# A decode block on one Trainium2 core: 128 columns of the first weight load move to a transfer of their own

## The chip, the cores and the metric

The kernel runs on one NeuronCore of one Trainium2 chip. The metric is the device time of one execution in microseconds (us), the median of several runs. A profile is one further execution, taken by the hardware profiler. The core has five instruction engines (PE for matmuls, with PEld for its weight loads; DVE, ACT and POOL for vector work; SP, which here only issues transfers) and 16 DMA engines that carry all data between HBM and the core's SBUF.

## The reference

One decode step for two sequences (B = 2, model width D = 448). The input is layer-normalised, then it goes through attention over a cache (16 query heads, 8 key/value heads, 4096 positions, head width 256) and through a bilinear feed-forward; the attention's output is multiplied by the gate and added to the input. All data are float32.

```python
xn = _layernorm(x)
q = (xn @ wq).reshape(B, 1, 16, 256).transpose(0, 2, 1, 3)
k, v = [jnp.repeat(t, 2, axis=1) for t in (k_cache, v_cache)]      # (2, 8, 4096, 256) each
p = softmax(jnp.einsum("bhqd,bhkd->bhqk", q, k) * 256 ** -0.5)
s = jnp.einsum("bhqk,bhkd->bhqd", p, v).transpose(0, 2, 1, 3).reshape(B, 1, 4096) @ wo
g = silu(((xn @ w_gate) * (xn @ w_up)) @ w_down)                    # inner width 1792
return x + s * g
```

The caches alone are 134 MB, the weights another 24 MB, and each byte is used once.

## The kernel before

**Data.** The host lays every array out as 128 rows, one for each SBUF partition, so that a load is 128 rows of one length. SP issues the loads in a fixed order, written out in `gated_decode_block` as a list of plans (lines 281 to 290): `wq0` (the first half of the query weights, 128 rows of 7168 columns = 28,672 bytes), `wgu` (gate and up weights), `wdq` (down weights and second half of the query weights), `first` (keys of the first head and sequence), then 14 loads `vk` of 128 rows of 65,536 bytes (values of one head and sequence, keys of the next), with `wo` after the second of them, and at the end `last0` in two pieces and `last1` in five, the last three of which are 5, 2 and 1 blocks of 448 columns of the output weights. The first four are issued at once; every later one waits until PE has done with the buffer it overwrites. There are two ring buffers and one slot.

**Work.** `query(0)` multiplies the normalised input by `wq0`: 14 blocks of 512 columns, the helper `rows` takes 12 of them in a first loop and the blocks 12 and 13 in a second one, so that block 13 is read by the last of its matmuls. `ffn_in`, `ffn_out` and `query(1)` follow. Then, for each head and sequence: scores, softmax, values. At the end `project` and `project_last` multiply by the output weights; `project_last` for the last eight chunks reads the last three pieces of `last1` as they land. Two DVE operations and the store of the result close the kernel.

**Recording.** The operations are not issued as they are written. `Recorder` notes them, `Flow.settle` works out from the regions that they read and write which must wait for which, and `Flow.issue` writes them out for each engine, with one semaphore for each transfer. So all instructions stand on the lines of that helper (line 220) in the profile, and are told apart by the tiles' names: `ring<-wq` is the load of `wq0`, `s<-ring,xnT` and `s<-ring,oT` are matmuls of `rows` (and of `project_last`, near the end).

Of the kernel before, what the change touches and what calls it, by code (L numbers as in the profile page):

```python
# [22 lines left out]
EPS = 1e-5  # L23
WQ = 14 * 512
LEAD = 48


class Flow:
# [115 lines left out]
    def issue(self):  # L144
        nc = self.nc
        lead = nc.alloc_semaphore("lead")
        for _ in range(LEAD):
            nc.vector.sem_inc(lead)
# [72 lines left out]
        return add  # L221


def gated_decode_block(nc, x, first, vk, last0, last1, wq0, wdq, wo, wgu, out):
    flow = Flow(nc)
    PE, DVE, ACT, POOL, SP = [getattr(flow, e) for e in ("PE", "DVE", "ACT", "POOL", "SP")]
    names = iter(range(1000))
# [35 lines left out]
    def issue(n=1):  # L263
        for names, place, src, cuts in todo[:n]:
            t = place()
            width = ROW if not names[0].startswith("w") else src.shape[1] // len(names)
            for i, name in enumerate(names):
                loaded[name] = t[:, i * width:(i + 1) * width]
            if names == ["wd", "wq1"]:
                loaded["wd"], loaded["wq1"] = t[:, :14 * D], t[:, 14 * D:]  # L270
            for lo, hi in zip(cuts, cuts[1:]):
                SP.dma_start(t[:, lo:hi], src[:, lo:hi])
        del todo[:n]

    def plan(names, place, src, cuts=None):
# [13 lines left out]
    plan(f"k{LAST + 1} v{LAST}", ring, last0, [0, ROW, 2 * ROW])  # L289
    plan(f"v{LAST + 1} wo2", ring, last1, [0, 6144, ROW, *(ROW + i * D for i in (5, 7, 8))])  # L290
    issue(4)


# [230 lines left out]
    for first in range(0, LAST, B):  # L524
        flow.turn = first
        issue(2)
        if first == 0:
            flow.turn = None
            issue()
            flow.turn = first  # L530
        for i in range(first, first + B):
            p = softmax(i, s)
            o = bank("o")
            values(i, p, o)
            DVE.tensor_copy(ob[:, i % B], o)
            q = copy()
            POOL.tensor_copy(q, query_of(i + 1))
            s = scores(i + 1, q, two())
        total(add_head)
        cb = combine(ob)  # L540
        t = work["h"]()[:, :B * 64]
        DVE.tensor_tensor(t.rearrange("p (s k) -> p s k", s=B), cb.rearrange("p (s k) -> p s k", s=B),
                          over[:, :, None].to_broadcast([128, B, 64]), op=OP.mult)
        turn(oT, first // B, t)
# [19 lines left out]
    t = work["h"]()  # L564
# [62 lines left out]
```

## Time and profile before

| | |
|---|---|
| median of 3 runs | 374.49 us (374.22 to 374.6) |
| the profiled execution's own time | 374.3 us |
| its span, from the first to the last instruction | 372.7 us |
| mean granted TensorE clock | 0.766 of full speed |
| PE busy, DVE busy, ACT busy | 188.0, 75.5, 26.7 us |
| moved by DMA | 158.67 MB, 426 GB/s over the span |

Times in views are counted from the first instruction. The profiled execution's own time is 1.6 us more than its span: work ahead of the first and behind the last instruction. A DMA share is the time of all packets that start in a stretch, divided by 16 engines times the stretch; in a stretch shorter than a packet it goes over 100%, and it then gives the packet's own duration (share x 16 x stretch). Every transfer is cut into packets, here one for each row, plus one packet of 4 bytes on each engine that took part, which counts up the semaphore.

### The profile page before, as it was taken

Reading aid. Unit: us, or ns where it says so; the run is one execution under the profiler, and the core shown is the slowest. Engines: PE = TensorE matmul, PEld = TensorE weight load, DVE = VectorE, ACT = ScalarE, POOL = GpSimd, SP = SyncE. Lnnn points to the kernel's source line nnn. Section 1 sums busy time; section 2 is a strip of 40 time slices with the busy share of each in tenths; the row PEclk is TensorE's granted clock in tenths of the full one; section 3 lists DMA queues with packets and bytes.
Section 4 is the critical chain, followed back from the end, with each engine's and each line's share of the span. In section 5 each row is a group of like instructions: output and inputs, shape, how many; then the busy total and the mean of one; then the engine's idle time right before and its main releaser. Section 6 shows DMA issues by size and latency. Waiting matters only on the chain. (4 is left out here: it accounts for less than half of the span.)

```text
span 372.7 us, 3346 instructions
## 1 busy us (share of the span) xinstructions
PE 188.0 (50%) x1474; PEld 57.2 (15%) x1474; DVE 75.5 (20%) x124; ACT 26.7 (7%) x44; POOL 5.6 (2%) x28
## 2 busy tenths in 40 slices
PE   0818292171900626555453638271919090908786
PEld 0201020020200201111121102020202030202223
DVE  2101013021130030313031212221131304030430
ACT  1101011001010010101000000101010101010121
POOL 0100000000000000000000000000000000000000
PEclk9968598596875685958595958695867586776999
DMA  8999999999999999999999999999999999999995
GB/s 339 466 424 410 429 433 450 443 445 396 425 459 436 450 443 436 429 394 450 436 450 443 436 429 394 450 436 450 443 436 429 394 450 436 450 397 443 421 414 233
DMA packets 3897, 158.67 MB, mean 426 GB/s; under 512 B 562, under 2 KB 692, under 8 KB 820
## 3 DMA queue, kind: packets, MB, share of 16 engines
q1 hardware_dynamic: 3888, 158.59, 98.6%
q8 instruction: 4, 0.07, 0.1%
q14 instruction: 1, 0.01, 0.0%
q10 hardware_dynamic: 4, 0.00, 0.0%
HBM read 158.54 MB, written 0.06 MB: 426 GB/s over the span
## 5 line engine op out<-in xcount | busy, mean ns | idle before, releaser
L220 PE MATMUL o<-ring,pT 128*32 128x512 f32 x480 | 81.4, 840 | 115.3 <-PEq L172 115.3
L220 PE MATMUL s<-ring,qc 128*32 128x512 f32 x448 | 50.7, 592 | 0.0
L220 PEld LDWEIGHTS o<-ring,pT 128*32 128x32 f32 x480 | 20.7, 149 | 163.5 <-issue 163.5
L220 DVE COPY ob<-o 128x512 f32<-128x512 f32 x14 | 9.7, 692 | 155.9 <-PE o L220 155.9
L220 ACT ACTIVATE p<-s,m 128x1024 f32<-128x1024 f32 x16 | 17.8, 1113 | 287.5 <-DVE m L220 287.5
L220 DVE TENSOR_REDUCE m<-s 128x1 f32<-128x1024 f32 x16 | 19.3, 1205 | 21.9 <-PE s L220 21.9
L220 DVE STREAM_TRANSPOSE pT<-p 128x1024 f32<-128x1024 f32 x15 | 18.7, 1245 | 19.1 <-ACT p L220 19.1
L220 PEld LDWEIGHTS s<-ring,qc 128*32 128x32 f32 x448 | 15.1, 110 | 33.0 <-issue 33.0
L220 PE MATMUL sm<-ident,m 128*1 128x128 f32 x16 | 4.3, 269 | 25.6 <-PEq L172 23.7
L220 PE MATMUL s<-ring,xnT 128*32 128x448 f32 (+1 forms) x72 | 12.1, 828 | 8.3 <-DMA ring<-wgu 8.3
L220 DVE TENSOR_REDUCE mx<-sm 1x128 f32<-1x512 f32 x16 | 10.9, 679 | 8.0 <-PE sm L220 8.0
L220 PE MATMUL sm<-one,mx 1*128 1x1 f32 x16 | 3.2, 198 | 12.9 <-PEq L172 12.1
L220 PE MATMUL s<-slot,hT 128*32 128x448 f32 x28 | 5.4, 885 | 8.0 <-DMA slot<-wdq 8.0
L220 POOL COPY qc<-qT 128x64 f32<-128x64 f32 x14 | 3.2, 236 | 290.9 <-PE s L220 283.6
L220 PE MATMUL s<-ring,qT 128*32 128x512 f32 x64 | 7.5, 597 | 0.0
L220 PEld LDWEIGHTS sm<-ident,m 128*1 128x1 f32 x16 | 1.3, 79 | 35.1 <-issue 32.9
L220 DVE RECIPROCAL over<-sm 128x2 f32<-128x2 f32 x8 | 1.4, 170 | 23.9 <-PE sm L220 23.9
L220 PE MATMUL s<-ident,pT 2*128 2x2 f32 x4 | 0.6, 247 | 10.5 <-DVE pT L220 10.5
L220 PE MATMUL cb<-ob,add_blocks 128*32 128x128 f32 x128 | 5.2, 279 | 0.6 <-ACT ob L220 0.6
L220 PEld LDWEIGHTS s<-ring,xnT 128*32 128x32 f32 x72 | 2.6, 145 | 17.0 <-DMA ring<-wgu 9.2
L220 PE MATMUL s<-ring,oT 128*32 128x112 f32 (+2 forms) x76 | 5.1, 314 | 0.1
L220 PE MATMUL wide<-slot,oT 128*32 128x448 f32 x48 | 4.9, 539 | 0.0
(65 smaller groups left out, 60.9 us busy)
## 6 DMA issues: line engine op xcount, KB each, us to landing
ring<-last SPq DMA_DIRECT2D x2, 4096.0 KB, 26.3
slot<-wdq SPq DMA_DIRECT2D x1, 6720.0 KB, 42.2
ring<-wgu SPq DMA_DIRECT2D x1, 6272.0 KB, 26.0
slot<-wo SPq DMA_DIRECT2D x1, 5376.0 KB, 46.6
ring<-first SPq DMA_DIRECT2D x1, 4096.0 KB, 51.2
ring<-wq SPq DMA_DIRECT2D x1, 3584.0 KB, 11.7
ring<-last SPq DMA_DIRECT2D x1, 3072.0 KB, 21.1
ring<-last SPq DMA_DIRECT2D x1, 1120.0 KB, 23.7
```

What stands on the lines that cost most here:

```text
L220: self.flow.record(self.engine, lambda: method(out, *args, **kw), writes, reads, name == "dma_start")
```

## The change

The last 128 of the 7168 columns of `wq0` leave its rows, which become 28,160 bytes long. They come as an array of their own, `wqx`, which is 4 groups of 33 rows of 128 columns, the 33rd row of each group being padding that is never read. Right behind the load of `wq0`, and ahead of `wgu`, SP issues one more transfer: 4 groups of 32 rows of 512 bytes into the same 128 columns of the same tile. Bytes read and their places in SBUF are the same as before.

```diff
+SHARE = 4
+COLS = 128
...
+            if names == ["wq0"]:
+                width = WQ
...
             for lo, hi in zip(cuts, cuts[1:]):
                 SP.dma_start(t[:, lo:hi], src[:, lo:hi])
+            if names == ["wq0"]:
+                SP.dma_start(t[:, cuts[-1]:WQ], wqx[:, :128 // SHARE])
...
     wq0, wq1 = [folded(wq[:, h], 512) for h in range(2)]
+    wqx = np.zeros((SHARE, 128 // SHARE + 1, COLS), np.float32)
+    wqx[:, :-1] = wq0[:, WQ - COLS:].reshape(SHARE, 128 // SHARE, COLS)
+    wq0 = c(wq0[:, :WQ - COLS])
```

## Rows read from the trace of the kernel before

**Rows 1.** Page, DMA busy share in 40 slices (tenths), and the queues.

```profile
DMA  8999999999999999999999999999999999999995
q1 hardware_dynamic: 3888, 158.59, 98.6%
q8 instruction: 4, 0.07, 0.1%
```

**Rows 2.** The chain that ended last, in order of time: start us, us, what.

```profile
344.56 23.68 DMA ring<-last
...
368.28 2.14 PE s L220 x64
...
370.44 0.29 DVE gate L220
```

**Rows 3.** Timeline from 368 us: start us, us, what, in brackets idle before and releaser.

```profile
368.28 0.92 PEld L220 LDWEIGHTS s<-ring,oT 128*32 128x32 f32 x40 [0.34 <-DMA ring<-last]
...
369.43 0.35 PEld L220 LDWEIGHTS s<-ring,oT 128*32 128x32 f32 x16 [0.23 <-DMA ring<-last]
369.97 0.16 PEld L220 LDWEIGHTS s<-ring,oT 128*32 128x32 f32 x8 [0.19 <-DMA ring<-last]
```

**Rows 4.** Windows near the end: stretch, busy by engine, PE clock, DMA share, GB/s.

```profile
366.00:367.50 1.50, 0.94 (x16) 0.25 (x8) 0.00 (x0) 0.68 (x1) 0.00 (x0) 1.00 0.99 400
367.50:368.00 0.50, 0.44 (x16) 0.38 (x16) 0.00 (x0) 0.01 (x1) 0.00 (x0) 1.00 0.98 373
```

**Rows 5.** The same view in shorter stretches behind it.

```profile
368.30:368.50 0.20, 0.20 (x9) 0.20 (x13) 0.20 (x1) 0.00 (x0) 0.00 (x0) 1.00 0.45 179
...
368.70:368.90 0.20, 0.20 (x20) 0.20 (x16) 0.00 (x0) 0.00 (x0) 0.00 (x0) 1.00 0.27 108
...
369.10:369.30 0.20, 0.20 (x16) 0.10 (x5) 0.00 (x0) 0.00 (x0) 0.00 (x0) 1.00 0.25 99
369.30:369.40 0.10, 0.10 (x8) 0.00 (x0) 0.00 (x0) 0.00 (x0) 0.00 (x0) 1.00 0.19 72
...
369.50:369.60 0.10, 0.10 (x8) 0.10 (x12) 0.00 (x0) 0.00 (x0) 0.00 (x0) 1.00 0.01 0
```

**Rows 6.** Queues, 350.2 to 350.3 us: packets, MB, share of 16 engines.

```profile
q8 instruction: 1, 0.02, 55.1%
```

**Rows 7.** Queues, 351.09 to 351.10 us.

```profile
q1 hardware_dynamic: 1, 0.03, 1101.2%
```

**Rows 8.** Queues, 351.14 to 351.16 us.

```profile
q1 hardware_dynamic: 1, 0.03, 379.1%
```

**Rows 9.** Windows, from 200 to 345 us.

```profile
200.00:345.00 145.00, 77.67 (x572) 23.56 (x576) 30.66 (x45) 8.43 (x14) 1.42 (x6) 0.75 0.99 431
```

**Rows 10.** Queues, 371.8 to 373 us: the store, 128 rows of 448 bytes.

```profile
q1 hardware_dynamic: 144, 0.06, 17.2%
```

**Rows 11.** Queues, 369.10 to 369.34 us: rows of 1792 bytes.

```profile
q1 hardware_dynamic: 13, 0.02, 25.1%
```

**Rows 12.** Queues, 5.5 to 6.7 us: q10 carries one row of the input x.

```profile
q10 hardware_dynamic: 2, 0.00, 0.4%
```

**Rows 13.** Timeline of SP's issues.

```profile
0.74 0.38 SPq L220 DMA_DIRECT2D ring<-wq  x1
1.17 0.42 SPq L220 DMA_DIRECT2D ring<-wgu  x1
...
35.89 22.13 SPq L220 DMA_DIRECT2D ring<-vk  x2
```

**Rows 14.** Timeline of PE's weight loads from 12 to 28 us.

```profile
12.71 0.20 PEld L220 LDWEIGHTS s<-ring,xnT 128*32 128x32 f32 x8 [1.29 <-DMA ring<-wq]
...
17.82 0.20 PEld L220 LDWEIGHTS s<-ring,oT 128*64 128x64 f32 x4 [1.50 <-issue]
27.22 0.20 PEld L220 LDWEIGHTS s<-ring,xnT 128*32 128x32 f32 x8 [9.21 <-DMA ring<-wgu]
```

**Rows 15.** Waits of SP: what waited for what, us in total, times, longest.

```profile
SPq L191 <- DMA res<-gate: 1.1, 1, 1.1
```

More of the change, by code (lines that the diff above doesn't have):

```diff
@@ L221, in __getattr__, with gated_decode_block @@
         return add
-def gated_decode_block(nc, x, first, vk, last0, last1, wq0, wdq, wo, wgu, out):
+def gated_decode_block(nc, x, first, vk, last0, last1, wq0, wqx, wdq, wo, wgu, out):
     flow = Flow(nc)
@@ L619 @@
     nc = bacc.Bacc("TRN2", target_bir_lowering=False, num_devices=1, dynamic_dma_scratch_size=1024)
-    arrays = dict(x=x, first=first, vk=vk, last0=last[0], last1=last[1], wq0=wq0, wdq=wdq, wo=wo, wgu=wgu)
+    arrays = dict(x=x, first=first, vk=vk, last0=last[0], last1=last[1], wq0=wq0, wqx=wqx, wdq=wdq, wo=wo, wgu=wgu)
     args = [nc.dram_tensor(n, a.shape, mybir.dt.from_np(a.dtype), kind="ExternalInput").ap()
```

## Prediction

> **What bounds the kernel now.** I read the page's first two parts and its queues, then the chain that ended last, then the end of the timeline, and then the DMA share in short windows, since what ends last turned out to be a transfer.
>
> The 16 DMA engines are the bound: their busy share stands at nine tenths or more in all slices but the first and the last, and SP's queue alone takes 98.6% of the span [rows 1]. PE, with 188 us of 372.7, waits for data. The chain of waits says where the end comes from: it lies on the transfers of `ring<-last` up to 368.23 us, then on the last 64 matmuls and two DVE operations [rows 2]. The timeline shows that these matmuls are still fed by transfers: the weight loads at 369.43 and 369.97 were each released by `ring<-last` [rows 3]. So the end stands at a fixed distance behind the landing of the last row of the last piece.
>
> That row lies on one engine, and the 16 do not end together. Between 366 and 368 us all are busy (share 0.99 and 0.98) [rows 4]. Then the share falls to 0.45, 0.27 and 0.25, which is four engines of 16; to 0.19, three engines, from 369.3 on; and to nothing after 369.5 [rows 5]. So some ten engines have ended by 368.3, four go on for more than a microsecond, one of these ends at about 369.35 and three at about 369.5. Bytes are no reason, since each 128-row transfer gives every engine eight rows. What differs is four packets of instructions, 0.07 MB in all [rows 1]. One of them took 55.1% x 16 x 0.1 us = 0.88 us [rows 6]. A data packet that begins as it ends took 1101.2% x 16 x 0.01 = 1.76 us [rows 7], where its neighbour of the same size took 379.1% x 16 x 0.02 = 1.21 [rows 8]: 0.55 more. Together that is 1.43 us on one engine, and 1.4 is just how far the four lag behind those that end near 368. So four engines each carried one instruction packet, and the kernel ends when the last of them does. That each of the four packets fell on another engine I infer from the four late ends.
>
> **What the change removes.** Each row of `wq0` loses 512 bytes; an engine's eight rows lose 4096. In the long stretch the queue moved 431 GB/s at a share of 0.99 [rows 9], that is 431 / 16 / 0.99 = 27.2 bytes a nanosecond on one engine. So each of the 16 saves 4096 / 27.2 = 0.15 us. Nothing hides this: the streams have no gap in which it could vanish, so an engine that is given nothing back ends 0.15 us sooner.
>
> **What it adds: 128 rows of 512 bytes.** First, on how many engines. The store, 128 rows, shows 144 packets [rows 10]: 128 rows and 16 completions, so 16 engines. One row of `x` shows two [rows 12]: one row and one completion, one engine. The new transfer has 4 groups at its outer level on one side and 128 rows on the other. The bounds are 4 engines with 32 rows each and 16 with eight; I take 4, since the outer count is what decided in both cases that the rows show, and keep 16 as a rival.
>
> The Trainium skill, DMA: Bandwidth & Descriptors, section "Why a DMA increments its semaphore by 16 and not by 1", says that the number of engines is the largest one up to 16 that divides the outer count of both sides, and that they are the lowest-numbered: 4 here, with the engine of the `x` rows among them. The two counts above agree with it; a transfer of 4 groups no row shows. By it the rival of 16 would fall away.
>
> Then, what one row of 512 bytes takes. From below: 512 / 27.2 = 19 ns, a piece of a long row. From above: a row of 1792 bytes, 25.1% x 16 x 0.24 us / 13 = 74 ns [rows 11]. The nearest row is the store's 448 bytes: 17.2% x 16 x 1.2 us / 144 = 23 ns a packet [rows 10], though that one writes to HBM and this one reads. On the line between 448 and 1792 bytes, 512 bytes take 25 ns; I take that. So 32 x 25 = 0.80 us for each of the four engines, net 0.80 - 0.15 = +0.65 us (bounds 0.45 and 2.22). The completion packet is hidden in the rounding.
>
> **What of it lies on the path.** The other 12 engines gain 0.15. If one of the three that end near 369.5 is among the four, the end moves by +0.65; if only the one that ends near 369.35, by about 0.15 less, +0.5. If none of the late four is among them, an engine that ends near 368.1 moves to 368.8, still ahead of the late ones, and the end moves by -0.15. Which four engines it is no view tells, since the rows carry no engine's number. By count alone, the chance that four engines out of 16 miss four given ones is (12 x 11 x 10 x 9) / (16 x 15 x 14 x 13) = 0.27, so 0.73 that a late one is hit.
>
> **What it moves at the start.** SP issues one transfer more, 0.4 us as its neighbours [rows 13], and `wgu` goes out at about 1.6 instead of 1.17. That is hidden behind the load of `wq0`, which lands only shortly before PE begins at 12.71 [rows 14]; without that cover it would cost 0.4. Only block 13 reads the new columns, in the last matmuls of `query(0)`, whose weight load stands at 17.82 [rows 14]; the new transfer lands within a microsecond of the old one. Behind these PE is idle for 9.21 us until `wgu` lands [rows 14], so even a wait there is hidden. `wgu` may land 0.65 us later if its slowest engine is one of the four; then PE, and behind it the issue of the first `vk` at 35.89 [rows 13], come 0.65 later. The queue still holds all of `first` at that time, 128 rows of 8192 columns, 4.2 MB or 9.7 us at 431 GB/s, so no engine runs dry. Later issues wait for PE in the same way, behind a load in flight.
>
> **Sum.** Own time 374.3, plus 0.65, or 0.5 if only the earlier of the late four is hit: 0.6 as a middle, 374.9. The median of the runs stands 0.19 above the profiled execution, so on it the same sum gives 375.1. Changes under 0.2%, 0.75 us, are about what a measurement of this kernel can't tell from none.
>
> **The rivals.**
>
> - *None of the late four is hit* (-0.15): 374.15 on the own time, 374.34 on the median. For it: 12 of 16 engines are early and have 1.2 us to spare [rows 5], more than the 0.65. Against it: 0.27 by count. It would be no measurable change either.
> - *The transfer spreads over 16 engines*, so the change does not do what it says: 8 x 25 ns = 0.20 added and 0.15 removed everywhere, 374.35. For it: the SBUF side still has 128 rows. Against it: the engines went by the count of 1 in the `x` rows.
> - *Slower, by the price of a small read.* If rows of 512 bytes from HBM take as long as those of 1792, 74 ns, a late engine that is hit ends 2.2 us later: 376.5, or +0.6%. An early one would end near 370.2, +0.7 us. This decides as soon as a late engine is hit and a row takes over (0.75 + 0.15) / 32 = 28 ns, or 33 ns on the earlier one, not far from my 25. For it: no row shows a read that small. Against it: the price falls with size down to 448 bytes, if only for writes.
> - *A small transfer stops the queue.* The store took 1.1 us by itself from its issue to its completion [rows 15]. If each engine paused so long around the new transfer, all 16 would lose 1.1 - 0.15: 375.25, slower by 0.25%. Against it: the seven pieces of the end follow each other at shares of 0.99 and 0.98 [rows 4]. The Trainium skill, DMA: Bandwidth & Descriptors, section "Rules for kernel authors", warns that under 64 KB a transfer is mostly overhead, and this one is 64 KB. By its table in "Measured", 64 KB take 0.95 us, which would make the sum 375.1. The trace does not bear that out for transfers queued behind others.
>
> **How the numbers follow.** Late engine hit, at some 25 ns a row: 0.53. None hit: 0.20. Sixteen engines: 0.05. Small reads dear, on a late engine: 0.14. The queue stops: 0.03. What is left, 0.05, is that the instruction packets fall elsewhere, or take less room, in the new program: I give 0.04 of it to a gain over 0.2%, which no price above reaches, and 0.01 to a loss. Faster is then 0.04, within 0.2% 0.53 + 0.20 + 0.05 = 0.78, slower 0.14 + 0.03 + 0.01 = 0.18. The likeliest gives 374.9, with a range of its own from 374.7 to 375.25 (the lower bound of the row's price on the own time; +0.75 on the median). The whole range runs from 374.1, where none is hit, to 375.4, which takes in the stopped queue and the dear reads up to some 33 ns a row.
>
> **What would show it.** In the profile after: some 0.06 MB of packets under 2 KB behind `wq0`, 128 of them with 4 completions (16 if it spreads), in some 25 ns each; the last weight load at 370.5 instead of 369.97 if a late engine is hit, at 369.8 if none is; the share near the end at about four engines still, three of them ending earlier by 0.15. The wait for `wgu` stays in place of any wait for the new transfer. The prediction is wrong if the rows of 512 bytes take over 30 ns, if the instruction packets move to other engines or times, or if the end moves by more than its slowest engine does.

## The result, and the profile after

The median of 22 runs is 374.95 us, beside 374.48 us for 22 runs of the kernel before in the same comparison. The ratio is 1.0041, with a 95% interval from 1.0024 to 1.0058: slower by 0.4%, where no measurable change was forecast. The ratio gives the high runs a weight that they do not have in a median; the two runs at 381.78 and 382.88, over 1.5% above the fastest, count as a slower state and are left out of it. The median lies within 0.05 us of the predicted 374.9, but for another reason. Of the 22 runs 12 lie between 374.46 and 374.97 us, with a median of 374.69; the other ten lie at 378.0 or above (six at 378.0 to 378.3, two near 379, and the two just named). All 22 of the kernel before lie between 374.22 and 375.41. So two things are to be explained: some 0.2 us in the lower runs, and 3.5 us or more in the others.

The profiled execution is one of the first kind: 374.64 us, with a span of 372.9. The lines of the helper stand two lines further down (222 instead of 220). Its queues on the page:

```profile
DMA packets 4029, 158.67 MB, mean 425 GB/s; under 512 B 566, under 2 KB 824, under 8 KB 952
...
q1 hardware_dynamic: 4020, 158.59, 98.6%
```

SP's queue has 4020 packets instead of 3888 [rows 1]: 132 more, 128 rows and 4 completions. So four engines carry the new transfer. Its packets, in a stretch in which only one engine still works on it:

```profile
q1 hardware_dynamic: 15, 0.01, 7.2%
```

That is the queue view from 12.34 to 12.69 us. 7.2% x 16 x 0.35 us / 15 = 27 ns for a packet, and 0.35 / 15 = 23 ns from one start to the next, since each begins a little before its predecessor ends. The price of 25 ns was right for most rows. Twelve of the 128, between 11.58 and 12.34 us, took 61 to 102 ns, most of them on the engine that was last to finish. From 11.85 to 12.30:

```profile
q1 hardware_dynamic: 7, 0.00, 7.7%
```

That is 7.7% x 16 x 0.45 us / 7 = 79 ns. The issues of SP, in its timeline:

```profile
0.74 0.38 SPq L222 DMA_DIRECT2D ring<-wq  x1
1.18 0.69 SPq L222 DMA_DIRECT2D ring<-wqx  x1
1.94 0.64 SPq L222 DMA_DIRECT2D ring<-wgu  x1
2.62 0.52 SPq L222 DMA_DIRECT2D slot<-wdq  x1
```

The new issue takes 0.69 us, not 0.4 as its neighbours did [rows 13], and the next ones are longer too. All of it ends long before `wq0` has landed, so it is hidden. The chain of waits ends as before, on `ring<-last` and the last 64 matmuls [rows 2]:

```profile
344.64 23.98 DMA ring<-last
...
368.66 2.05 PE s L222 x64
...
370.73 0.29 DVE gate L222
```

The last weight load in the timeline stands at 370.26 instead of 369.97 [rows 3], 0.29 later:

```profile
368.66 1.39 PEld L222 LDWEIGHTS s<-ring,oT 128*32 128x32 f32 x56 [0.35 <-DMA ring<-last]
...
370.26 0.16 PEld L222 LDWEIGHTS s<-ring,oT 128*32 128x32 f32 x8 [0.21 <-DMA ring<-last]
```

And the windows near the end, as [rows 4, 5]:

```profile
367.50:368.00 0.50, 0.07 (x4) 0.07 (x8) 0.00 (x0) 0.38 (x1) 0.00 (x0) 1.00 0.90 348
368.30:368.50 0.20, 0.20 (x12) 0.01 (x1) 0.00 (x0) 0.00 (x0) 0.00 (x0) 1.00 0.59 233
368.70:368.90 0.20, 0.20 (x12) 0.20 (x16) 0.20 (x1) 0.00 (x0) 0.00 (x0) 1.00 0.28 108
369.10:369.30 0.20, 0.20 (x20) 0.20 (x13) 0.00 (x0) 0.00 (x0) 0.00 (x0) 1.00 0.32 125
...
369.50:369.60 0.10, 0.10 (x16) 0.08 (x4) 0.00 (x0) 0.00 (x0) 0.00 (x0) 1.00 0.14 54
369.70:369.80 0.10, 0.10 (x12) 0.10 (x8) 0.00 (x0) 0.00 (x0) 0.00 (x0) 1.00 0.09 36
```

The share falls earlier (0.90 where it was 0.98) and ends later: after 369.5, where nothing was left before, two engines still work, and one after 369.7. It looks like the step that was forecast, an engine that ends late and has got more to carry. The packets say otherwise. The queue view names no engine, but a packet begins some 4 ns before the one ahead of it on its engine ends, so the packets of the trace can be strung into 16 sequences. The first row of 512 bytes begins at 10.97 us, so an engine with 32 of them, 23 ns apart, can't be done before 11.70. Four engines begin `wgu` later than that, at 11.73, 11.79, 11.82 and 12.72; they end at 368.68, 368.72, 368.75 and 369.65. The last to end, at 369.95, is none of these: it began `wgu` at 11.48 and carried the instruction packet at 78.45. In the kernel before, the packet at 78.12 fell on an engine that began `wgu` at 11.22, and that one ended last too, at 369.57. The two packets (78.44 to 78.45 us, and before, 78.11 to 78.12):

```profile
q8 instruction: 1, 0.02, 624.4%
q8 instruction: 1, 0.02, 596.2%
```

and the first row of `wgu` on the engine that carried each (11.480 to 11.481, and before, 11.221 to 11.222):

```profile
q1 hardware_dynamic: 1, 0.05, 12006.2%
q1 hardware_dynamic: 1, 0.05, 11581.2%
```

So the end moved because one instruction packet fell on an engine that stood 0.26 us further behind, with a first row of `wgu` 0.07 us longer, and not because the last engine had small rows to carry. Nothing in this trace hints at 378 us.

### The profile page after: what moved, and what is told of

The parts are those of the page before. It is cut to its first block, busy times and chain, and to the rows that moved or that the text cites. A ratio compares the mean times of both kernels' runs of the same rounds, so it can differ in the third digit from the quotient of the medians.

```text
span 372.9 us, 3347 instructions
## 1 busy us (share of the span) xinstructions
PE 192.0 (51%) x1474; PEld 58.1 (16%) x1474; DVE 75.5 (20%) x124; ACT 26.8 (7%) x44; POOL 5.6 (2%) x28
## 3 DMA queue, kind: packets, MB, share of 16 engines
q1 hardware_dynamic: 4020, 158.59, 98.6%
## 5 line engine op out<-in xcount | busy, mean ns | idle before, releaser
L222 PE MATMUL o<-ring,pT 128*32 128x512 f32 x480 | 86.0, 881 | 110.6 <-PEq L174 110.6
L222 PEld LDWEIGHTS o<-ring,pT 128*32 128x32 f32 x480 | 21.5, 154 | 161.5 <-issue 161.5
```

Source lines behind the costliest of these rows:

```text
L222: self.flow.record(self.engine, lambda: method(out, *args, **kw), writes, reads, name == "dma_start")
```

## The experiments

The theories, as the expectations name them. **A**: in some runs the small rows are dear. **B**: in some runs all engines read slower, because arrays lie badly in HBM. **C**: four engines that stand 0.6 us behind the others bring this about. **D**: the sizes of the arrays shift the places of those behind them. **E**: the small rows on few engines bring it about, by whatever means; **E1**: that the engines are few, **E2**: that one engine's small rows are many. Each run of five rounds gives 10 to 12 times; "high" means 377 us or more. The diffs show the lines that matter and leave out the rest. No run of the kernel before, of the 22 and another 155 beside the experiments, was over 375.6.

**The change again, its 16-engine form, another place, eight groups.**

```diff
 e2_sixteen, e12_sixteen_again
+    wqx = c(wq0[:, WQ - COLS:])
+                SP.dma_start(t[:, cuts[-1]:WQ], wqx)
 e3_behind_wgu
-            if names == ["wq0"]:
-                SP.dma_start(t[:, cuts[-1]:WQ], wqx[:, :128 // SHARE])
+            if names == ["wg", "wu"]:
+                SP.dma_start(ring.bufs[1][:, WQ - COLS:WQ], wqx[:, :128 // SHARE])
 e4_eight
-SHARE = 4
+SHARE = 8
```

> The changed kernel once more, unaltered. Of 22 runs of it, 12 lay at 374.5 to 375.0 us and the others at 378 or above, while all 22 of the kernel before lay at 374.2 to 375.4. Theory A (price): in some executions the rows of 512 bytes are read at over 100 ns instead of 24 to 27, so one of the four engines ends some 3.7 us later; runs at 378 come again, in about 4 of 10, and if the profile is of such a run the new transfer's last completion lands near 16 us instead of 13.2. Theory B (rate): the arrays lie elsewhere in HBM, or the engines stand otherwise to each other, and all 16 move data 1% slower through the whole run; then a profile at 378 shows some 421 GB/s in every slice and a landing of the new transfer at 13 us. Rival: the runs at 378 were no property of the kernel; then all lie at 374.5 to 375.0.

Measured: 2 of 11 high (377.87, 378.28), the others with a median of 374.84; ratio 1.0026 (1.0006 to 1.0047). The high runs belong to the kernel.

> The same 128 columns in a transfer of their own at the same place, but as 128 rows of 512 bytes at the outer level, so that 16 engines carry eight rows each. By my sum: 0.2 us added and 0.15 removed on each engine, so 374.5, the kernel before within 0.1%. Theory A: a read of 100 ns costs at most 0.8 us on an engine, so no run over 375.5. Theory B by addresses: the arrays behind wq0 are displaced here too, so runs at 378 come as often as with the change. Theory B by the engines' standing: no run at 378, since all engines are shifted alike.

Measured: 0 of 11 high, 374.56 to 375.70; ratio 1.0016 (1.0007 to 1.0025). The page counts 4032 packets on SP's queue, 144 more than before, so 16 engines.

> The new transfer, unaltered in shape, is issued behind wgu instead of ahead of it, so that the engines read it at 26 us and not at 11, among rows of 53,760 bytes. Last matmuls of query(0) wait until 27 us for it, which PE's idle time there hides. Theory A with a price that comes from the place near the start: no runs at 378, 374.7 to 375.0. Theory A with a price of any small read: runs at 378 as often as with the change. Theory B: as often as with the change.

Measured: 1 of 10 high, at 377.36, the others with a median of 375.0; ratio 1.0024 (1.0010 to 1.0038). The place at the start is not what matters. This one run lies 2.4 us above the others and not 3.5; with only `wdq` behind the small rows that would fit the row times below (8 x 0.24 = 1.9 us), but no profile shows it.

> 8 groups of 16 rows of 512 bytes: by the counts, eight engines carry 16 rows each, 16 x 24 ns = 0.38 us added and 0.15 removed, net +0.23 on these and -0.15 on the other eight. My sum: 374.3 to 374.8. Theory A: at 130 ns a row some runs at 376.3 instead of 378 (half the rows on an engine, half the delay). Theory B: the second group stays at 378.

Measured: 4 of 12 high (378.25, 378.37, 380.35, 382.81), the others with a median of 374.76; ratio 1.0018 (1.0000 to 1.0036). Half the rows on an engine do not halve the delay, against A. The profiled execution is the one at 378.25, with a span of 376.6, and shows where it comes from. From the transfers' view of this kernel (issue to landing, us, at the end of each line):

```profile
q1 hardware_dynamic: 4024, 158.59, 98.5%
...
slot<-wdq SPq DMA_DIRECT2D x1, 6720.0 KB, 44.8
ring<-wgu SPq DMA_DIRECT2D x1, 6272.0 KB, 27.4
...
ring<-first SPq DMA_DIRECT2D x1, 4096.0 KB, 53.8
ring<-wq SPq DMA_DIRECT2D x1, 3520.0 KB, 11.4
```

The same view of the changed kernel:

```profile
slot<-wdq SPq DMA_DIRECT2D x1, 6720.0 KB, 41.2
ring<-wgu SPq DMA_DIRECT2D x1, 6272.0 KB, 26.0
...
ring<-first SPq DMA_DIRECT2D x1, 4096.0 KB, 50.3
ring<-wq SPq DMA_DIRECT2D x1, 3520.0 KB, 11.2
```

`wq0` lands 0.2 us later, `wgu` 1.4 us later, `wdq` 3.6 us later, and `first` 3.5: next to nothing is lost before, and nothing more after. The windows over these loads and over the long stretch of values and keys, eight groups:

```profile
14.00:24.00 10.00, 4.67 (x28) 0.90 (x20) 0.90 (x2) 0.21 (x1) 0.41 (x2) 0.98 1.04 401
30.00:40.00 10.00, 8.25 (x56) 1.86 (x48) 1.27 (x2) 1.81 (x2) 0.00 (x0) 0.81 0.97 376
...
110.00:345.00 235.00, 117.18 (x841) 35.40 (x845) 48.87 (x73) 14.45 (x24) 2.37 (x10) 0.71 1.00 433
```

and the changed kernel:

```profile
14.00:24.00 10.00, 4.92 (x28) 0.79 (x17) 0.90 (x2) 0.10 (x1) 0.41 (x2) 0.84 1.00 432
30.00:40.00 10.00, 6.14 (x48) 1.42 (x40) 1.27 (x2) 1.81 (x2) 0.00 (x0) 0.95 1.00 435
...
110.00:345.00 235.00, 120.16 (x872) 36.27 (x876) 47.96 (x71) 13.25 (x22) 2.36 (x10) 0.72 1.00 434
```

All engines are busy in both (share near 1), but 401 and 376 GB/s flow where 432 and 435 did; later both are alike. Single rows in the queue view of eight groups, in order a row of `wgu` (14.33 to 14.34 us), one of `wdq` (43.06 to 43.07), the last one of `wdq` (44.42 to 44.43) and one of `first` (46.35 to 46.36):

```profile
q1 hardware_dynamic: 1, 0.05, 1299.4%
q1 hardware_dynamic: 1, 0.05, 1393.1%
q1 hardware_dynamic: 1, 0.05, 1315.0%
q1 hardware_dynamic: 1, 0.03, 761.9%
```

and of the changed kernel, a row of `wgu` (14.9 to 14.92) and one of `wdq` (30.3 to 30.32):

```profile
q1 hardware_dynamic: 1, 0.05, 579.1%
q1 hardware_dynamic: 1, 0.05, 620.3%
```

So a row of `wgu` took 2.08 us instead of 1.85, one of `wdq` 2.23 instead of 1.99, both 12% longer. The trace has all 256 rows of the two loads. The first row of `wgu` on each engine, begun while the small rows were being read, took 1.87 to 1.97 (on one engine 2.62); from the second on, every row took 2.08, and every row of `wdq` 2.19 to 2.23 but the very last. That one, for about half of whose time the other engines had gone on to `first`, took 2.10, and a row of `first` 1.22, against 1.21 in the changed kernel. Seven rows of `wgu` and eight of `wdq` on each engine make 7 x 0.23 + 8 x 0.24 = 3.5 us, the distance between the groups. It is the loads behind the small rows that are slow, on all engines, and not the small rows, which took 27 ns here: A falls. Of the changed kernel itself no high run was profiled; that its runs at 378.0 to 378.3 come about in the same way is argued from their equal distance.

**Is it where arrays lie?**

```diff
 e5_shift (kernel before; wgu by 16 words, wdq 64, wo 128, first 512)
+        arrays[n] = np.concatenate([np.zeros(k, np.float32), arrays[n].reshape(-1)])
+            args[i] = args[i][shift[n]:].rearrange("(p n) -> p n", p=128)
 e6_inside (the change)
+    wq0=np.concatenate([wq0.reshape(-1), wqx.reshape(-1)])     # no array wqx
 e7_extra, e13_extra64k (kernel before)
+    wqx=np.zeros((4, 33, 128), np.float32)                     # e13: (4, 32, 128)
+    ACT.dma_start(extra, wqx[0, :1])
 e8_last (the change)
+    arrays = dict(..., wdq=wdq, wo=wo, wgu=wgu, wqx=wqx)
 e11_stride (the change)
+        arrays[n] = np.pad(arrays[n], ((0, 0), (0, 2 * ROW - w)))    # wgu, wdq
 e14_even (the change)
+    wqx = np.zeros((SHARE, 3 * 128 // SHARE, COLS), np.float32)
 e15_sixteen_odd (e2_sixteen)
+    wqx = np.concatenate([wq0[:, WQ - COLS:], np.zeros((128, COLS), np.float32)])
```

> The kernel before; only the places of four arrays in HBM differ: the rows of wgu begin 64 bytes further on, those of wdq 256, those of wo 512 and those of first 2048 bytes, each behind a lead of zeros in its own array. In the 378 us run of eight groups the rows of wgu (50,176 bytes) took 2080 ns instead of 1853 and those of wdq (53,760) 2227 instead of 1985, every one of them, with wo and the keys unaffected. Theory B1 (place by small offset): a base that is not a multiple of some power of two costs this 12%; then one or more of the four arrays show rows longer by 12%, wgu before all. Theory B2 (place in another sense: which memory or bank an array gets when it is loaded): all rows keep their times, 374.3 to 375.

Measured in a single execution: 374.98 us; `wgu` landed after 26.2 us (26.0 before), `wdq` 42.8 (42.2), `first` 51.8 (51.2), with rows of 1.85 and 1.99 us. B1 as stated, a cost in every run, falls for these offsets; one that comes in a quarter of the runs could have been missed.

> The changed kernel with the new array appended to wq0's own array, so that the program has as many arrays as the kernel before; transfers and rows are those of the change. If the runs at 378 come from one more array among the inputs (B2), they are gone and all runs lie at 374.5 to 375.1 (or 375.7 when two instruction packets meet on one engine). If they come from the small rows on four engines, or from the shortened rows of wq0, about a quarter of the runs lies at 378 again.

Measured: 4 of 12 high (378.05 to 378.46), the others with a median of 374.64; ratio 1.0038 (1.0012 to 1.0064). The number of arrays is not it.

> The kernel before with one more input array of the size of the new one, of which a single row of 512 bytes is read at the start into a place of its own; its 128-row loads are unaltered. B2 by number of arrays: about a quarter of the runs at 378, though not one byte of the loads has moved. Price of small rows, or an effect of the shorter rows: all runs at 374.2 to 375.4 as the kernel before.

Measured: 0 of 12 high, 374.27 to 375.94; ratio 1.0000 (0.9992 to 1.0009).

> The changed kernel with the new array as the last in the list of inputs instead of between wq0 and wdq. If wgu and wdq are slow in some runs because the new array stands ahead of them, the runs at 378 are gone: 374.5 to 375.1. If they come from the transfer itself or from the number of arrays, about a quarter lies at 378 again.

Measured: 1 of 12 high (378.47), median of the others 374.73; ratio 1.0014 (0.9997 to 1.0031). The place in the list is not it.

> The changed kernel with the rows of wgu and wdq at a distance of 65,536 bytes in HBM, as those of the values and keys are, instead of 50,176 and 53,760 end to end; the bytes read are the same. Theory C with the distance of the rows as its second condition: no run at 378. Theory C without it: about a quarter of the runs at 378. If a distance of 65,536 is bad for these lengths, all runs are slower.

Measured: 2 of 12 high (379.29, 382.85), the others with a median of 374.92; ratio 1.0021 (1.0000 to 1.0042). The distance of the rows is not a condition.

> The kernel before with one more input array of 65,536 bytes, one row of which is read at the start. Theory D (place in HBM): with wq0 shorter by one unit of 65,536 bytes and the new array taking two, all forms that had runs at 378 take an odd number of such units more or less than the kernel before, and the forms that had none an even number (0 or 2); this one is odd with the loads of before, so a quarter of the runs at 378. Theory E (the transfer of small rows on few engines): none, 374.2 to 375.9.

Measured: 0 of 12 high, 374.21 to 375.30; ratio 0.9999 (0.9990 to 1.0008).

> The changed kernel with the new array padded to three units of 65,536 bytes (only the first 32 rows of each group of 96 are read), which makes the displacement even. Theory D: no run at 378, 374.5 to 375.5. Theory E: about a quarter at 378.

Measured: 5 of 12 high (378.19 to 378.51), the others with a median of 374.85; ratio 1.0045 (1.0017 to 1.0073).

> The 16-engine form, which had no run at 378 in 22, with its array padded to two units of 65,536 bytes, so that the displacement is odd. Theory D: about a quarter at 378. Theory E: none, 374.5 to 375.7.

Measured: 11 runs from 374.71 to 375.65, none at 378. A twelfth, at 393.91 with TensorE's granted clock at 0.552 in it, can't be judged by its time; in its trace too the rows of `wgu` took 1.85 us and those of `wdq` 1.99. D fails in all three of its forecasts.

**Is it unequal engines, or the small rows?**

```diff
 e9_ahead (kernel before; e10_behind: if names == ["wd", "wq1"])
+            if names == ["wq0"]:
+                SP.dma_start(ring.bufs[1][:16, WQ + ROW:],
+                             first.rearrange("(g r) n -> g r n", g=4)[:, :4, :1024])
 e16_rows_alone (kernel before)
+            if names == ["wq0"]:
+                again = first.rearrange("p n -> (p n)")[:4 * 33 * 128].rearrange("(g r c) -> g r c", g=4, c=128)
+                SP.dma_start(ring.bufs[1][:, WQ + ROW:WQ + ROW + 128], again[:, :32])
 e17_eight_rows (as e16)
+                SP.dma_start(ring.bufs[1][:32, WQ + ROW:WQ + ROW + 128], again[:, :8])
 e18_all_rows (as e16, again in four pieces of 128 rows)
+                for j in range(4):
+                    SP.dma_start(ring.bufs[1][:, WQ + ROW + 128 * j:WQ + ROW + 128 * (j + 1)], again[j])
```

> The kernel before, with its rows of wq0 as they were, and one more transfer ahead of wgu: 4 groups of 4 rows of 4096 bytes, read a second time from the keys into a place that nothing reads. By the counts four engines carry 16 KB each, some 0.62 us, as much as the small rows of the change cost them. Theory C (unequal engines): what makes the weights' rows slow in some runs is that four engines stand 0.6 us behind the others when wgu begins; then some runs lie at 378, the rest at 374.5 to 375.2. Theory A (small rows, or the shortened rows of wq0): no run at 378.

Measured: 0 of 11 high, 374.21 to 375.28; ratio 0.9999 (0.9990 to 1.0008). The page counts 3908 packets, 16 rows and 4 completions more than before. C falls, as far as 11 runs can tell.

> The same transfer as in the last one, behind wdq instead of ahead of wgu. Theory C: wgu and wdq are read as in the kernel before, so no run at 378; the end is as there, 374.5 to 375.2, since the four engines carry the same bytes. If a displaced set of engines slows any load that follows, runs at 378 or above come here too, with other rows than wgu's and wdq's slow.

Measured: 0 of 11 high, 374.32 to 375.23; ratio 0.9999 (0.9990 to 1.0008).

> The transfer over 16 engines once more, unaltered: none of its first 11 runs lay over 375.7. Theory C: again none, 374.5 to 375.7. If the runs at 378 come from the shortened rows of wq0 or from one more transfer of small rows as such, in a quarter of the runs, then 11 without one were luck (chance 0.04) and some come now.

Measured: 0 of 11 high, 374.54 to 375.67; ratio 1.0011 (1.0002 to 1.0019).

> The kernel before with its arrays and loads, and a transfer of the change's shape ahead of wgu: 4 groups of 32 rows of 512 bytes, read a second time from the keys into a place that nothing reads. Theory D: no run at 378; four engines carry 0.77 us more than before, 374.5 to 375.6. Theory E: about a quarter at 378.

Measured: 4 of 12 high (377.83, 377.98, 378.80, 382.50), the others with a median of 374.53; ratio 1.0026 (1.0000 to 1.0053). The transfer alone does it, with the arrays, the rows of `wq0` and all other loads of the kernel before: E.

> The kernel before with a transfer ahead of wgu of 4 groups of 8 rows of 512 bytes, read a second time from the keys into a place that nothing reads: four engines carry eight small rows each, 0.19 us. Theory E1 (few engines): some of the runs at 378. Theory E2 (many small rows in one engine's queue): none, 374.3 to 375.6.

Measured: 0 of 11 high, 374.25 to 375.54; ratio 0.9998 (0.9988 to 1.0007).

> The kernel before with four transfers of 128 rows of 512 bytes ahead of wgu, read a second time from the keys into places that nothing reads: every engine carries 32 small rows, 0.77 us more on all, so 375.1 to 376.2 without anything else. Theory E1: nothing above that. Theory E2: a quarter of the runs 3.7 us higher, near 379.

Measured: 0 of 12 high, 375.02 to 376.33, median 375.33; ratio 1.0025 (1.0015 to 1.0034), which is about what 32 x 24 ns on every engine cost. Neither E1 nor E2 holds alone.

Together: with 16 or 32 rows of 512 bytes on eight or four engines, ahead of a load of weights, 33 of 115 runs were high; without the six above 380 us it is 27 of 109. None was with eight such rows on 16 engines (33 runs, without the one set aside) or on four (11), with 32 on 16 engines (12), or with 16 KB in longer rows on four engines (22). At 25% a run, 11 without a high one are luck in 0.75 to the 11th = 0.04 of cases, 33 in less than one of 10,000.

## Why the prediction was wrong

The step that failed is in "What of it lies on the path": it gave each engine the bytes and rows of its own and let every other load keep its rate of 27.2 bytes a nanosecond. None of the rivals had another load slowed. In 10 of 22 runs the kernel loses 3.5 us or more; in the one profile of such a run, that of eight groups, the rows of the two loads behind are 12% longer on all 16 engines, and with all bytes on the path this shows in full. The range held the median only because 12 of 22 runs have none of it, which is luck.

A second step failed in the lower runs: that a late engine is among the four, and moves the end by +0.5 to +0.65. In the profiled execution the rival came true that none is hit, and its -0.15 did not show either, because an instruction packet moved to another engine, which the prediction itself named as a sign of being wrong. The profiles of the experiments bear this out. In all eleven kernels whose `wq0` has the shorter rows, the second of the four instruction packets (at 78.4 to 82.1 us) fell on an engine that had begun `wgu` at 11.48 to 11.91 us. In seven kernels with the rows of before it fell on one that had begun at 11.00 to 11.25 (the exceptions are e5, with 11.67, and e18, in which all engines begin later). The lowest times go with it: 374.46 to 374.71 against 374.19 to 374.44, and alike for four, eight and 16 engines. Only in e8 is the engine with that packet one of the four. So the +0.2 us belongs to what the forms with shorter rows share, and not to small rows on four engines; that it has the sign of the forecast is luck. Why the packet falls where it does, the runs do not tell.

Point by point. *Four engines* was right (132 packets more), and so were the 16 of the other form (144) and the eight of 8 groups (136). The rule of the Trainium skill that was weighed there, in DMA: Bandwidth & Descriptors, "Why a DMA increments its semaphore by 16 and not by 1", agrees with these three counts; that the engines are the lowest-numbered no run here shows. *25 ns a row* was right for most rows: 23 from start to start. *Four late engines, each with one instruction packet*, which the prediction inferred, holds: strung up, the four packets lie on four engines, before and after. *One of them is hit* was wrong, as said: +0.29 in the profile and +0.2 in the median of the runs under 377, where +0.5 to +0.65 was forecast, and from another cause. Extra bytes on four engines without small rows (e9, e10) cost nothing at all, and e16, with the same small rows, nothing in its runs under 377. *Hidden at the start* was right, even with an issue of 0.69 us. *A fixed cost that stops the queue* did not show: the 16-engine forms, of the same 64 KB, cost 0.07 to 0.16%, not 0.25%. They cost more than the 0.05 us of my sum, though, some 0.4 to 0.5 us by their medians. The instruction packet can account for a part (it fell on engines that began `wgu` at 11.55 to 11.79), and the medians mix two kinds of run, since the profiled one of e2, at 375.58, ends on matmuls that wait for no transfer, as do those of e9, e11, e14 and e17 at 374.99 to 375.51.

What stays open: by which mechanism many small rows on some of the engines slow the loads behind them. The trace of a high run suggests that it is not one engine's own pace, since the rows of `wdq` grow shorter as other engines leave that load (2.23, then 2.19 to 2.21, the last 2.10), so the engines may share something that is short. Why `wgu` and `wdq` suffer and `first` does not, and why it happens in one run and not in the next, the runs do not tell. Of the runs near 379 to 383 no profile was caught, so what they lose beyond the 3.7 us is open too. The other limit is chance: that e9, e17 and e18 never fall into it rests on 11, 11 and 12 runs. And e18 brought its 32 rows an engine in four transfers, so it is open whether the rows must be of one transfer.

No form beat the kernel before. The gain that could be had, 0.15 us on the engines that end last, is 0.04%.

## What to carry to other kernels

Where 16 DMA engines run without a gap, read the end by the DMA share in short windows: it shows how many engines end last, and a transfer's packets (rows plus one completion for each engine) show how many carry it. Which engine ends last can be read only by stringing its packets together, and an instruction packet on another engine moves the end by as much as a small change does. A transfer whose rows fall on a few of the engines is not priced by its own bytes: many small rows on four or eight of them, queued ahead of large loads, cost some 3.5 us in about a quarter of the runs here, and in the one that was profiled those loads were 12% slower. The same rows over all 16 engines never did this in 45 runs. One profile could not show it; a dozen plain runs beside the kernel before did.

## What the runs showed of the hardware that was not expected

A load of 128 rows can run at two rates in one and the same program: 27.1 bytes a nanosecond on an engine (50,176 bytes in 1.85 us) or 24.1 (in 2.08 us), on all engines at once. The slow rate was seen in one profile, from the second row of `wgu` on each engine to the end of `wdq`. How far the rows lie apart (50,176 or 65,536 bytes) made no difference to the high runs; arrays that begin 64 to 2048 bytes further on kept their row times, in the single execution that was run. And one packet of 16 KB of instructions costs the one engine that carries it 1.43 us, more than its own 0.88, because the engine's data stand still meanwhile and the data packet that begins as it ends is stretched as well [rows 6, 7, 8].
